# A Fourier filter feeding a two-layer product: 32 complex-product sums moved from GpSimd to VectorE, one step later

## The chip, the cores and the metric

The kernel runs on one core of a Trainium2 chip. Five engines work from their own instruction queues, each strictly in order, and wait for one another through semaphores: TensorE (PE in the profile; its weight loads are PEld), VectorE (DVE), ScalarE (ACT), GpSimd (POOL) and SyncE (SP), which here only issues transfers. Products are written to PSUM banks, which VectorE and ScalarE read; everything else lies in SBUF. The metric is the device time of one execution in microseconds (us).

## The reference

The input `x` is 8 batches of 3008 rows by 256 channels. The first half of the computation is a filter in the frequency domain, the second a two-layer product with a nonlinear step between:

```python
X = np.fft.rfft(x, axis=1)
Y = X * (filt_r + 1j * filt_i)[None]
y = np.fft.irfft(Y, n=3008, axis=1)
h = y.reshape(8 * 3008, 256) @ w_in          # 256 x 2048
out = (h - np.tanh(h)) @ w_out               # 2048 x 256
```

## The kernel before

**The transform.** 3008 is 64 times 47, and each transform is done as two small ones by matmul. `first` (line 338) does the 64-point part, `middle` (395) the 47-point part, the complex product with the filter and the 47-point part back, `last` (500) the 64-point part back. The batches go in five units: batch 0, the pairs (1, 2), (3, 4), (5, 6), and batch 7. Batch 0 is transformed in a prologue; every other unit is transformed piece by piece while the unit before it goes through the two-layer product. So `middle` of the first pair, unit 1, runs during the product of batch 0.

**One front step and one back step of `middle`.** For a pair there are 32 indices j. The front step of j (lines 424 to 448) multiplies a 128x512 tile `pz` on TensorE (L430). ScalarE makes `zs`, the two halves of `pz` swapped and one of them negated (L443, L444). VectorE makes `uv = pz * fr` (L445), GpSimd `zs = zs * fi` (L446) and then `uv = uv + zs` (L447). The back step `back()` of j multiplies `uv` again on TensorE into `pe` (L411), which ScalarE copies out (L414) and sends to memory. `uv` and `zs` have two buffers each. After the first index, fronts and backs alternate: front j, back j-1, front j+1, back j.

**The product.** Tokens come in groups of up to 512 columns, six groups for batch 0, and each group is worked through in four quarters of the 2048 hidden columns. A quarter is numbered U, and u is U modulo 4. Both products are done as two-by-two blocks with seven products and extra sums in place of eight products. In the round of quarter U, three things are interleaved: `up(U)` (532) forms the hidden tile `h` from the PSUM banks X, Y and Z; `shrink(U-1)` (607) applies the nonlinear step in two halves; `down(U-2)` (660) does the second product. The second half of `shrink` ends with a VectorE instruction (L633) and then `combine` (523): four GpSimd sums in a row, L524 to L527, that prepare the operand tiles of the second product. `last` of the next group uses the same `combine` lines for its tile `tu`.

**The order.** The schedule is written by hand: each engine takes its instructions in the order in which the Python code emits them. `up` has five places, called slots 0 to 4 here, where `t(k)` is called (for batch 0 these calls are lines 568, 578, 585, 594 and 602). A slot emits at most one step of `first` or `middle`, as the evenly spaced due times ask (line 1140); with u = 3, slots 0 and 2 are taken by `last` instead. The VectorE instructions of a round come in this order:

- slot 0, then L571 (the sum of Y and a copy of X), for u = 1 also L694, then L626 of the first half of `shrink`;
- slot 1, then L633 of the first half, for u = 1 also L700;
- slot 2, then L588, then L626 of the second half;
- slot 3, then L596 (the copy of X), then L633 of the second half, and with it the four GpSimd sums of `combine`; for u = 1 also L712;
- slot 4, then L604 (the sum into Z's share of `h`).

On TensorE, slot 1 lies behind the sixth product into X and slot 4 behind the fourth.

**The banks of the steps.** `pz`, `pe` and the other products of the steps have no bank of their own but take one of two, named "t" and "y" (line 1045). The bank "y" is also the Y of `up`:

```python
quarter, latest = [1], ["t"]
def zd(name, shape):
    latest[0] = "y" if quarter[0] in (1, 2, 3) and latest[0] == "t" else "t"
    return ps.tile(shape, F32, tag=latest[0], bufs=1, name=name)
```

`quarter[0]` is the number of the slot. A step in slot 0 or 4 takes "t", and the step in slot 1 then takes "y", which L571 must have read before.

Of the kernel before, what the change touches and what calls it, by code (L numbers as in the profile page):

```python
# [143 lines left out]
def kernel(  # L144
# [10 lines left out]
    V, G, ACT = nc.vector, nc.gpsimd, nc.scalar  # L155
# [13 lines left out]
    def dram(t, off, dims):  # L169
        return bass.AP(tensor=t, offset=off, ap=[list(d) for d in dims])  # L170
# [199 lines left out]
    def load_slots(j, pool=None):  # L370

        w = 4 * (128 + RP2)
        t = (tr.tile([IM + RP, 4, 128 + RP2], F32, tag="fg", bufs=2, name="fg") if pool is None else
             pool.tile([IM + RP, 4, 128 + RP2], F32, tag="a1", bufs=4, name="fg"))
        nc.sync.dma_start(t, fg_d[:, w * j:w * (j + 1)])
        return t[:, :, 0:128], t[:, :, 128:]

    def load_a2(p, j, filters=True, tag="a2"):

        t = tr.tile([RP2, 2 * BD], F32, tag=tag, bufs=2, name="a2")  # L380
        row = 32 * len(UNITS[p]) * DM
        nc.sync.dma_start(t, dram(ct1[p], 2 * j * BD, [[row, RP2], [1, 2 * BD]]))
        n = 2 if len(UNITS[p]) == 2 else 4
        if not filters:
            return t
        ft = tr.tile([128, 2, n, DM], F32, tag="ft", bufs=2, name="ft")
        for p0 in (0, IM):
            nc.sync.dma_start(ft[p0:p0 + IM], dram(filt_d, n * j * DM,
                                                   [[2 * NK * DM, IM], [NK * DM, 2], [1, n * DM]]))
        if n * (j + 1) == NK:  # L390
            nc.sync.dma_start(ft[IM:IM + 1, 0, n - 1, :],
                              dram(filt_r.tensor, SEQ // 2 * DM, [[DM, 1], [1, DM]]))
        return t, ft

    def middle(p, z):

        pair = len(UNITS[p]) == 2
        per = 1 if pair else 2
        n = NK // per
        w = BD // per  # L400
        a2 = {0: load_a2(p, 0)}
        mats = {0: load_slots(0)}
        waiting = []
        yield

        def back():
            j, uv = waiting.pop(0)
            pe = z("pe", [128, per, w])
            for i in range(per):
                k = per * j + i  # L410
                nc.tensor.matmul(pe[0:RP2, i], mats[k // 4][1][:, k % 4], uv[0:IM + RP, i],  # L411
                                 start=True, stop=True)
            e1 = tr.tile([RP2, 2, DM], F32, tag="e1", bufs=2, name="e1")
            ACT.copy(e1, pe[0:RP2])  # L414
            step = (NQ if pair else 2) * RP * DM
            ACT.dma_start(
                dram(ct2[p], per * j * RP2 * DM, [[DM, RP2], [step, 2], [1, DM]]), e1)

        for j in range(n):
            if j % 2 == 0 and j // 2 + 1 < n // 2:  # L420
                a2[j // 2 + 1] = load_a2(p, j // 2 + 1)
            k4 = per * j // 4
            if per * j % 4 == 0 and k4 + 1 < NK // 4:
                mats[k4 + 1] = load_slots(k4 + 1)
            pz = z("pz", [128, per, w])
            at, ft = a2[j // 2] if j % 2 == 0 else a2.pop(j // 2)
            for i in range(per):
                k = per * j + i
                lo = j % 2 * BD + i * w
                nc.tensor.matmul(pz[:, i], mats[k // 4][0][0:R2, k % 4],  # L430
                                 at[0:R2, lo:lo + w], start=True, stop=True)

            uv = tr.tile([128, per, w], F32, tag="uv", bufs=2, name="uv")
            zs = tr.tile([128, per, w], F32, tag="zs", bufs=2, name="zs")
            lo = j % 2 * per
            fr, fi = (ft[:, v, lo:lo + per, :] for v in range(2))
            if pair:
                fr, fi = (f.to_broadcast([128, 2, DM]) for f in (fr, fi))

            def rows(t):  # L440
                return t.rearrange("p i (b c) -> p (i b) c", c=DM)

            ACT.mul(zs[0:IM], pz[IM:128], -1.0)  # L443
            ACT.copy(zs[IM:128], pz[0:IM])  # L444
            V.tensor_mul(rows(uv), rows(pz), fr)  # L445
            G.tensor_mul(rows(zs), rows(zs), fi)  # L446
            G.tensor_add(uv, uv, zs)  # L447
            waiting.append((j, uv))
            yield
            if len(waiting) > 1:  # L450
                back()
                yield
        back()
        yield
# [401 lines left out]
    with tc.tile_pool(name="tr", bufs=2) as tr, tc.manual_schedule():  # L856
        with tc.tile_pool(name="pro", bufs=1) as pro, \
# [136 lines left out]
            for j in range(NK // 2):  # L994
# [13 lines left out]
                uv = tr.tile([128, 2, DM], F32, tag="uv", bufs=2, name="uv")  # L1008
                zs = tr.tile([128, 2, DM], F32, tag="zs", bufs=2, name="zs")
# [28 lines left out]
        with tc.tile_pool(name="dn", bufs=2) as dn, \  # L1038
# [48 lines left out]
            for U in range(total + 2):  # L1087
                i, u = divmod(U, 4)
                if U < total:
                    p, c = groups[i]  # L1090
# [36 lines left out]
                def t(k):  # L1127


                    nonlocal ms, done  # L1130
                    quarter[0] = k
                    if k == 2 and stores:
                        store(*stores.pop())
                    store_some(4)
                    if U >= total:
                        return
                    pos = 20 * c + 5 * u + k
                    if u == 3 and k in (0, 2) and i + 1 < len(groups):
                        next(lasts)
                    elif done < len(steps) and steps[done] <= pos:  # L1140
                        if done < n_f:
                            next(fs)
                        else:
                            next(ms)
                        done += 1
                        if done == n_f:
                            ms = middle(p + 1, z1)
                            next(ms)
                    next(late, None)
                    if U > 0 and k in (1, 3):  # L1150
                        next(copies, None)
# [56 lines left out]
```

## Time and profile before

| what | value |
|---|---|
| median of 3 runs (lowest to highest) | 2804.87 us (2803.72 to 2805.23) |
| the profiled execution: its time, its span | 2805.23 us, 2803.4 us |
| granted TensorE clock, mean over the span | 0.991 |
| busy share of the span: DVE, ACT, POOL | 68%, 67%, 63% |
| L445 in 240 to 480 us | 32 times, mean 686 ns |
| L446 in 240 to 480 us | 32 times, 47.5 us, mean 1483 ns |
| L447 in 240 to 480 us | 32 times, 59.5 us, mean 1861 ns |
| POOL idle before L524 in 240 to 480 us | 19.2 us, ended by L633 on DVE |

The 32 front steps of unit 1 lie between 238.8 and 467.1 us from the start of the span. A row of a timeline gives the start, the duration, the engine, the line, the tiles written and read, and in brackets the idle time of the engine before the row and what ended it. Matmuls are pipelined: a row of four 128x256 matmuls of which each starts 0.216 us after the one before is listed with 1.03 us, since the end of the last is counted too. TensorE is packed if the next row starts where this rate puts it, and the time lost is what the next row starts later. Each matmul of the code appears as two in the trace.

### The profile page before, as it was taken

Reading aid. Unit: us, or ns where it says so; the run is one execution under the profiler, and the core shown is the slowest. Engines: PE = TensorE matmul, PEld = TensorE weight load, DVE = VectorE, ACT = ScalarE, POOL = GpSimd, SP = SyncE. Lnnn points to the kernel's source line nnn. Section 1 sums busy time; section 2 is a strip of 40 time slices with the busy share of each in tenths; the row PEclk is TensorE's granted clock in tenths of the full one; section 3 lists DMA queues with packets and bytes.
Section 4 is the critical chain, followed back from the end, with each engine's and each line's share of the span. In section 5 each row is a group of like instructions: output and inputs, shape, how many; then the busy total and the mean of one; then the engine's idle time right before and its main releaser. Section 6 shows DMA issues by size and latency. Waiting matters only on the chain.

```text
span 2803.4 us, 36463 instructions
## 1 busy us (share of the span) xinstructions
PE 2715.9 (97%) x12438; PEld 2273.4 (81%) x12438; DVE 1912.5 (68%) x2175; ACT 1885.6 (67%) x2790; POOL 1767.5 (63%) x1407
## 2 busy tenths in 40 slices
PE   4799999999999999999999999999999999999998
PEld 2577778888888888888888888888888888898887
DVE  6756666566776777666677776766676676777776
ACT  2476777666767776666677777666666676666665
POOL 5546887544776777544576777654476666565655
PEclk7999999999999999999999999999999999999999
DMA  9754443322333222223323233112223222111010
GB/s 251 208 189 122 106 124 76 91 83 72 75 79 77 73 71 59 63 79 81 87 72 75 70 80 83 38 43 65 59 66 83 60 57 58 29 19 26 16 23 17
DMA packets 322591, 217.53 MB, mean 78 GB/s; under 512 B 224782, under 2 KB 274746, under 8 KB 322156
## 3 DMA queue, kind: packets, MB, share of 16 engines
q1 hardware_dynamic: 266826, 157.28, 23.6%
q10 hardware_dynamic: 52818, 51.53, 6.0%
q0 software_dynamic: 2752, 6.30, 0.8%
q8 instruction: 100, 1.64, 0.2%
q14 instruction: 95, 0.78, 0.1%
HBM read 138.87 MB, written 79.17 MB: 78 GB/s over the span
## 4 chain that ended last, share of the span: by engine, by line
PE 83%; DVE 5%; ACT 4%; DMA 3%; POOL 2%; issue 2%; ACTq 0%; SPq 0%; DVEq 0%; POOLq 0%
PE o L680 35%; PE x L545 21%; PE z L545 10%; PE y L545 5%; PE pe L411 3%; PE pz L430 3%; PE pu L511 3%; PE pf L351 2%; DVE h L626 2%; ACT y L622 1%; DVE h L596 1%; DMA raw<-in_moe_w_in_dram 1%; DMA filt<-in_filt_r_dram 1%; ACT y L619 1%; DVE h L633 0%
## 5 line engine op out<-in xcount | busy, mean ns | idle before, releaser
L626 DVE TENSOR_TENSOR h<-h,y 128x1024 f32<-128x1024 f32 (+2 forms) x384 | 577.4, 1504 | 311.5 <-ACT y L622 310.4
L680 PE MATMUL o<-t,wd 128*128 128x256 f32 (+2 forms) x3072 | 775.1, 375 | 1.8 <-POOL t L526 1.3
L680 PEld LDWEIGHTS o<-t,wd 128*128 128x128 f32 x3072 | 579.9, 190 | 92.9 <-issue 22.0
L633 DVE SCALAR_TENSOR_TENSOR h<-sq,h 128x1024 f32<-128x1024 f32 (+2 forms) x384 | 558.7, 1455 | 121.0 <-ACT sq L630 113.0
L524 POOL TENSOR_TENSOR t<-h 128x512 f32<-128x512 f32 (+2 forms) x192 | 240.2, 1251 | 552.0 <-DVE h L633 401.3
L545 PE MATMUL x<-tu,wu 128*128 128x256 f32 (+2 forms) x2304 | 582.4, 375 | 4.3 <-POOL tu L525 2.2
L680 PE MATMUL o<-h,wd 128*128 128x256 f32 (+2 forms) x2304 | 582.5, 375 | 4.0 <-DVE h L633 4.0
L545 PEld LDWEIGHTS x<-tu,wu 128*128 128x128 f32 x2304 | 430.9, 190 | 104.7 <-issue 42.4
L680 PEld LDWEIGHTS o<-h,wd 128*128 128x128 f32 x2304 | 430.7, 190 | 76.9 <-issue 15.8
L630 ACT ACTIVATE sq<-y,near_b 128x1024 f32<-128x1024 f32 (+2 forms) x384 | 435.0, 1133 | 6.4 <-DVE h L633 0.2
L619 ACT ACTIVATE y<-h 128x1024 f32<-128x1024 f32 (+2 forms) x384 | 397.4, 1035 | 14.4 <-ACT e L414 6.4
L622 ACT ACTIVATE y<-y 128x1024 f32<-128x1024 f32 (+2 forms) x384 | 399.9, 1041 | 6.6 <-ACT a L352 0.4
L551 ACT COPY s<-x 128x512 f32<-128x512 f32 (+2 forms) x192 | 110.8, 577 | 328.5 <-PE x L545 308.4
L527 POOL TENSOR_TENSOR t<-t,h 128x512 f32<-128x512 f32 (+2 forms) x192 | 318.9, 1661 | 0.1
L551 ACT COPY u<-x 128x512 f32<-128x512 f32 (+2 forms) x384 | 220.7, 575 | 138.2 <-PE x L545 119.9
L525 POOL TENSOR_TENSOR t<-h,t 128x512 f32<-128x512 f32 (+2 forms) x192 | 246.0, 1281 | 15.1
L526 POOL TENSOR_TENSOR t<-h 128x512 f32<-128x512 f32 (+2 forms) x191 | 245.6, 1286 | 0.0
L446 POOL TENSOR_TENSOR zs<-zs,ft 128x512 f32<-128x512 f32 x112 | 164.8, 1472 | 91.4 <-ACT zs L444 91.2
L447 POOL TENSOR_TENSOR uv<-uv,zs 128x512 f32<-128x512 f32 x112 | 206.7, 1846 | 9.1 <-DVE uv L445 0.5
L545 PE MATMUL x<-ut,wu 128*128 128x256 f32 (+2 forms) x768 | 198.6, 381 | 10.0 <-DVE h L596 8.3
L588 DVE TENSOR_TENSOR h<-z,u 128x512 f32<-128x512 f32 (+2 forms) x192 | 128.8, 671 | 112.6 <-ACT u L551 111.6
L545 PE MATMUL z<-tu,wu 128*128 128x256 f32 (+2 forms) x768 | 194.5, 376 | 0.0
(122 smaller groups left out, 3291.6 us busy)
## 6 DMA issues: line engine op xcount, KB each, us to landing
a<-ct SPq DMA_DIRECT2D x64, 384.0 KB, 3.8
ft<-filt SPq DMA_DIRECT2D x96, 256.0 KB, 4.5
out_dram<-ot SPq DMA_DIRECT2D x1392, 16.0 KB, 1.5
ct<-e ACTq DMA_DIRECT2D x112, 192.0 KB, 2.2
ct<-a ACTq DMA_DIRECT2D x80, 256.0 KB, 2.9
x_sb<-in_x_dram SPq DMA_DIRECT2D x69, 256.0 KB, 2.9
e<-ct SPq DMA_DIRECT2D x33, 512.0 KB, 4.3
fg<-fg SPq DMA_DIRECT2D x40, 392.0 KB, 4.9
```

The lines of the kernel that those rows point to most:

```text
L524: G.tensor_sub(t[0], b[0][1], b[0][0])
L525: G.tensor_sub(t[1], b[1][1], t[0])
L526: (V if shared else G).tensor_sub(t[2], b[1][1], b[0][1])
L527: G.tensor_sub(t[3], t[1], b[1][0])
L545: nc.tensor.matmul(bank[:, k], wu[:, q - 1, (2 * u + k) * 128:(2 * u + k + 1) * 128], rhs[q - 1], start=(first and k == 0), stop=True, ski ...
L551: ACT.copy(t, X)
L619: ACT.activation(y[k], ht[k], AF.Arctan, scale=S)
L622: ACT.activation(y[k], y[k], AF.Square, accum_out=y_sums[:, 2 * U + k // 2:2 * U + k // 2 + 1])
L626: V.tensor_mul(ht[k], ht[k], y[k])
L630: ACT.activation(sq[k], y[k], AF.Square, bias=near_b, scale=A)
L633: V.scalar_tensor_tensor(out=ht[k], in0=sq[k], scalar=K, in1=ht[k], op0=ALU.add, op1=ALU.mult)
L680: nc.tensor.matmul(product(q), wd[:, q - 1, (2 * u + k) * 128: (2 * u + k + 1) * 128], rhs[q - 1][:, k], start=(u == 0 and k == 0 and q == ...
```

## The change

In `middle` of unit 1 alone, GpSimd no longer adds `zs` to `uv`. The sum is kept back and emitted on VectorE: at the end of the next back step or, for the very first index, which has no back step after it, at the end of the second front step. The sums of the other units stay where they were.

```diff
@@ middle(p, z)
         waiting = []
+        late_add = p == 1
+        adds = []
         yield
...
             V.tensor_mul(rows(uv), rows(pz), fr)
             G.tensor_mul(rows(zs), rows(zs), fi)
-            G.tensor_add(uv, uv, zs)
+            if not late_add:
+                G.tensor_add(uv, uv, zs)
             waiting.append((j, uv))
+            if adds:
+                V.tensor_add(*adds.pop())
+            if late_add:
+                adds.append((uv, uv, zs))
             yield
             if len(waiting) > 1:
                 back()
+                if adds:
+                    V.tensor_add(*adds.pop())
                 yield
```

## The prediction

> **What bounds the kernel now.** I read the page first: busy shares, then the chain that ended last.
>
> ```profile
> PE 2715.9 (97%) x12438; PEld 2273.4 (81%) x12438; DVE 1912.5 (68%) x2175; ACT 1885.6 (67%) x2790; POOL 1767.5 (63%) x1407
> PE 83%; DVE 5%; ACT 4%; DMA 3%; POOL 2%; issue 2%; ACTq 0%; SPq 0%; DVEq 0%; POOLq 0%
> ```
>
> TensorE sets the time. A change on POOL and DVE counts only where TensorE then waits more or less than now. The change acts where the first pair's `middle` runs, 240 to 480 us, so I read the windows (busy time of PE, PEld, DVE, ACT, POOL) there and in the next stretch, and what TensorE waits for there.
>
> ```profile
> 240.00:480.00 240.00, 234.46 (x979) 179.19 (x978) 154.66 (x173) 175.10 (x267) 194.52 (x142) 1.00 0.44 113
> 480.00:720.00 240.00, 239.73 (x1119) 205.89 (x1118) 152.61 (x171) 162.52 (x240) 116.79 (x99) 1.00 0.29 78
> ```
> ```profile
> PE pe L411 <- POOL uv L447: 3.9, 2, 3.3
> PE pe L411 <- DVE h L571: 1.3, 6, 0.3
> ```
>
> POOL is the fullest of the helpers (194.5 of 240), yet TensorE waits for it twice only, at the first back step and near the end (470.16). Against the rate of 0.216 us a matmul these cost 3.48 and 0.72 us. So 4.2 us is all that a faster sum can give directly. The six waits for L571 are the second thing to see: a step in slot 1 uses bank "y" and cannot start until L571 has read it.
>
> Next, the timelines of TensorE, POOL and DVE at the start of round 9, the first round with u = 1 (start, duration, engine, line).
>
> ```profile
> 264.82 1.03 PE L545 MATMUL x<-tu,wu 128*128 128x256 f32 x4
> 265.69 1.02 PE L430 MATMUL pz<-a,fg 94*128 94x512 f32 x2
> 266.55 1.03 PE L545 MATMUL z<-tu,wu 128*128 128x256 f32 x4
> ```
> ```profile
> 260.73 1.27 POOL L524 TENSOR_TENSOR t<-h 128x512 f32<-128x512 f32 x1 [2.89 <-DVE h L633]
> 262.08 1.27 POOL L525 TENSOR_TENSOR t<-h,t 128x512 f32<-128x512 f32 x1
> 263.31 1.27 POOL L526 TENSOR_TENSOR t<-h 128x512 f32<-128x512 f32 x1
> 264.55 1.27 POOL L527 TENSOR_TENSOR t<-t,h 128x512 f32<-128x512 f32 x1
> 265.78 1.26 POOL L446 TENSOR_TENSOR zs<-zs,ft 128x512 f32<-128x512 f32 x1
> 267.12 1.27 POOL L447 TENSOR_TENSOR uv<-uv,zs 128x512 f32<-128x512 f32 x1
> ```
> ```profile
> 261.78 0.68 DVE L604 TENSOR_TENSOR h<-z,u 128x512 f32<-128x512 f32 x1
> 262.51 0.69 DVE L571 TENSOR_TENSOR h<-y,s 128x512 f32<-128x512 f32 x1
> 266.81 0.42 DVE L694 TENSOR_TENSOR o<-o,p 128x256 f32<-128x256 f32 x1 [3.61 <-ACT p L693]
> 267.15 2.32 DVE L626 TENSOR_TENSOR h<-h,y 128x1024 f32<-128x1024 f32 x1
> ```
>
> TensorE is packed here: 264.82, 265.69, 266.55 follow without a hole. The front step in slot 4 of round 8 put its POOL product (L446) behind the four sums of `combine`, emitted in that round's slot 3. It ends only at 267.04; DVE passes L571 at 262.51.
>
> **The change, part by part.**
>
> *Removed from POOL:* 32 sums, 59.5 us in the window. Worth 4.2 us at most, the two waits.
>
> *Added to DVE:* 32 sums of 128x512 with both inputs in SBUF. The trace has no such row. L445, as large, takes 0.69 us and the next instruction starts 0.61 later (261.17 to 261.78); L626, twice the size with both inputs in SBUF, takes 1.22 alone and hands over after 1.15 (273.39 to 274.54). I take 0.61. The bounds: 0.42, a 128x256 sum (L694), and 0.69 plus one POOL instruction of 1.27, because L626 beside L447 waited that one out:
>
> ```profile
> 256.57 1.27 POOL L447 TENSOR_TENSOR uv<-uv,zs 128x512 f32<-128x512 f32 x1
> ```
> ```profile
> 256.83 2.09 DVE L626 TENSOR_TENSOR h<-h,y 128x1024 f32<-128x1024 f32 x1 [0.31 <-ACT y L622]
> 258.84 0.68 DVE L596 COPY h<-x 128x512 f32<-128x512 f32 x1
> ```
>
> *The place of the sums.* Each waits for its own L446 and holds DVE until then. The step moves past the back step's matmul, ScalarE copy and the store issued on ScalarE; no transfer moves, and neither SP nor POOL gets a new wait.
>
> - Slots 1 to 4 (27 sums): L446 is done or nearly done, and L626 loses the POOL sum that slowed it, 2.09 to about 1.22. In round 8, slot 3, DVE then runs L626 256.83, sum 257.98, L596 258.59 instead of 258.84. Where L626 was not slowed (290.73, 1.20 us), L596 ends at 293.1 and X is needed at 294.09. The sums in slot 1 stand before L633, which waits for ScalarE (316.87 for L626, 319.85 for L633). In slot 4 they delay L604, whose bank is refilled about 5 us later. I cost these at nothing; the cover is this slack, 1 us before L596, and if it went, each would cost up to 0.9 (1.88 minus 1.0).
> - Slot 0 of rounds 9, 13, 17 and 21 (u = 1): the sum stands before L571, L694 and L626. In round 9 it starts where L447 did, 267.12; L571 starts at 267.73 and ends at 268.42; the matmul follows 0.14 later (as 282.68 to 282.82), at 268.56 instead of 265.69: 2.87. The four POOL sums start 0.26 earlier, as L596 and so L633 do (the 0.25 above, rounded with the handover): 2.61. Round 13 the same (333.97; `pz` 332.54): 2.60. Round 17 (400.87; 399.45): 2.59. Round 21 (468.10; L571 0.62; 466.09) 3.38, less 0.45 because L626 in round 20 took 2.27: 2.93, and the 0.72 wait that followed it goes: 2.21. DVE's own 3.61 us of idle before L694 hides the wait from L694 and L626, but TensorE needs L571 long before that.
> - The first index: its sum stands in slot 0 of round 8 before L571. L446 ends at 246.82 and POOL goes straight to the next L446. If the sum slips in ahead, `pe` starts at 248.34 instead of 249.22 (gain 0.9); if it waits that product out, L571 ends near 249.3 and `pe` starts about 0.2 late. I take the second, since POOL needs no signal between its two products.
>
> *Sum:* 2.61 + 2.60 + 2.59 + 2.21 + 0.2 = 10.2 us on the profiled execution of 2805.23 (span 2803.4). That run lies 0.36 above the median, so 2804.87 + 10.2 = 2815.1. What waits on TensorE elsewhere follows it and shifts along.
>
> [...] POOL's sum takes 1861 ns on the mean, DVE's product 686. [...]
>
> **The rivals.**
>
> 1. *No wait at L571* (not slower): the POOL waits go and nothing takes their place: -4.2, 2800.7; with the waits for L571 (six of about 0.37) and three of 0.36 behind L596 gone as well, -7.6, 2797.3. It decides if L446 ends before DVE reaches slot 0, at 262.5. It ends 4.5 us later and the sums before it start only after L633. Chance 0.07.
> 2. *The wait is there but hits no one:* if the step in slot 1 held bank "t", L571 could be late. Then only the ends change: 0.2 minus 0.72, 2804.4. Against it, the six waits of `pe` for L571. Chance 0.04.
> 3. *DVE becomes the bound:* the other sums do not hide. With the POOL block, seven in slot 3 at 0.9 give 6.3 more, 2821; all 27 others at 0.61 give 16.5, 2832. For it, L626 already suffers from POOL; against it, DVE is at 64% and loses the neighbour that slowed it. Chance 0.10.
>
> **How the numbers follow.** Forecast 0.79. Its own bounds: a sum of 0.42 (-0.8), twice the head start (-1.2), a gain at the first index (-1.1) give 7.1; a POOL block at each of four sites (+5.1) and no head start (+1.2) give 16.5. The range 2809 to 2820 leaves rivals 1 and 2, most of 3 and the far end of the forecast out, about 0.2. A measurement of this kernel can tell 0.2% (5.6 us). Rival 1 gives faster 0.03 and no change 0.04, rival 2 no change 0.04; the rest is slower, 0.89.
>
> **What would show it.** In the changed profile: four waits of `pz` (L430 before, a few lines lower after) for L571, about 2.6 us each, one per group; DVE idle about 4.5 us before the new sum in slot 0, ended by POOL's L446; no wait of TensorE for the POOL sum; L626 near 1.2 to 1.4; PE busy in the same stretch of work 6 us or more below its length. The forecast is wrong if those four waits are missing, or if TensorE waits behind L596 or L633 instead.

## The result and the profile after

The changed kernel takes 2820.7 us (median of 6 runs, 2819.3 to 2821.2) against 2805.6 us for the kernel before (6 runs, 2803.7 to 2812.2): the ratio is 1.0050, with a 95% interval of 1.0037 to 1.0063. That is 15.1 us more, by the interval 10.4 to 17.7. The direction and the mechanism came as forecast. The size did not quite: 10.2 us were forecast, and 2820.7 lies 0.7 us above the upper end of the range. The profiled executions show the same, 2821.2 against 2805.23 us.

In the changed kernel's file the lines have moved a little: L411 is now L414, L430 L433, L446 L449, L571 L581, L626 L636; the new sum is L461, and L454 for the first index. In the other runs they differ again by a few lines. The page of the changed kernel, its first line and its chain:

```profile
PE 2723.6 (97%) x12438; PEld 2278.4 (81%) x12438; DVE 1923.2 (68%) x2207; ACT 1886.2 (67%) x2790; POOL 1706.5 (61%) x1375
PE 73%; DVE 4%; ACT 3%; issue 2%; POOL 1%; ACTq 0%; DVEq 0%; POOLq 0%
```

POOL has lost 61 us of work and DVE has gained 11 us, and the kernel is slower: neither share says anything about the time. In the stretch of the change, taken to 492 us here since its work ends later (the columns are the busy times of PE, PEld, DVE, ACT and POOL, then the granted TensorE clock, the DMA share and GB/s), and in what TensorE waits for there:

```profile
240.00:492.00 252.00, 238.22 (x968) 180.80 (x967) 164.49 (x203) 173.40 (x264) 131.15 (x107) 0.98 0.42 106
```
```profile
PE pz L433 <- DVE h L581: 9.5, 4, 2.5
PE pe L414 <- DVE h L581: 3.9, 4, 3.4
```

POOL falls from 194.5 to 131.2 us, and TensorE no longer waits for it. In its place stand four waits of `pz` for L581 (L571 before), one in each round with u = 1. Beside them there is something that no line of the profile before had in this stretch: a granted clock of 0.98, not 1.00.

The start of round 9 on TensorE, POOL and DVE (start, duration, engine, line):

```profile
267.43 1.03 PE L555 MATMUL x<-tu,wu 128*128 128x256 f32 x4
270.67 1.12 PE L433 MATMUL pz<-a,fg 94*128 94x512 f32 x2 [2.22 <-DVE h L581]
271.63 1.55 PE L555 MATMUL z<-tu,wu 128*128 128x256 f32 x4
272.98 1.06 PE L690 MATMUL o<-h,wd 128*128 128x256 f32 x2
```
```profile
266.79 1.28 POOL L537 TENSOR_TENSOR t<-t,h 128x512 f32<-128x512 f32 x1
268.02 1.27 POOL L449 TENSOR_TENSOR zs<-zs,ft 128x512 f32<-128x512 f32 x1
```
```profile
269.32 0.69 DVE L461 TENSOR_TENSOR uv<-uv,zs 128x512 f32<-128x512 f32 x1 [4.31 <-POOL zs L449]
269.93 0.68 DVE L581 TENSOR_TENSOR h<-y,s 128x512 f32<-128x512 f32 x1
270.53 0.42 DVE L704 TENSOR_TENSOR o<-o,p 128x256 f32<-128x256 f32 x1
270.86 1.22 DVE L636 TENSOR_TENSOR h<-h,y 128x1024 f32<-128x1024 f32 x1
```

DVE stands idle for 4.31 us in front of the sum, L581 comes behind it, and `pz` 0.06 us after L581 has ended. Then comes what was not forecast: from 271.63 the same matmuls take 1.55 and 1.06 us where they took 1.03 and 0.60 before. The second of these before:

```profile
267.41 0.60 PE L680 MATMUL o<-h,wd 128*128 128x256 f32 x2
```

Three stretches of the changed kernel show why; the figure behind the busy times is the granted clock:

```profile
251.52:254.93 3.41, 3.41 (x10) 2.70 (x9) 1.23 (x2) 2.91 (x4) 0.00 (x0) 0.50 1.02 235
272.00:275.41 3.41, 3.41 (x10) 2.70 (x9) 1.42 (x3) 3.37 (x5) 1.27 (x1) 0.50 0.23 52
411.95:415.36 3.41, 3.41 (x10) 2.70 (x9) 1.42 (x2) 3.37 (x5) 1.27 (x1) 0.50 0.22 47
```

After three of the five long waits the granted clock is 0.50 for 3.41 us, and each of these stretches shows TensorE as fully busy.

**Where the time went.** Both kernels give TensorE the same 12438 matmuls in the same order, so the start of the same matmul in the two traces tells how far the changed kernel is behind. At 233.4 us it is 0.85 us behind, at 494.8 us 14.61, and that stays within 0.05 until 2716 us. The change thus cost 13.8 us in this stretch and nothing later. The other 2.2 us of the 16.0 between the two profiled executions lie in the prologue and at the very end. The change does not act there, and the prologue differs between executions of one kernel: in the first run of the experiments the changed kernel is 0.81 us ahead of the kernel before at 233.4 us. Taken apart, with the time lost against the rate of 0.216 us a matmul (each of the four waits includes 0.10 us that the second matmul of `pz` starts late behind it):

| step of the sum | forecast, us | measured, us |
|---|---|---|
| first back step (3.48 us of wait before, 3.58 now) | +0.2 | +0.1 |
| waits for L571 in rounds 9, 13, 17, 21 | +2.61, +2.60, +2.59, +2.93 | +2.48, +2.62, +2.61, +2.80 |
| wait of the back step in round 21 that goes | -0.72 | -0.79 |
| shorter waits for L571 and L596 elsewhere | 0 | about -1.1 (the rest of the balance) |
| halved clock, three stretches | not in the sum | +1.68, +1.68, +1.68 |
| sum | +10.2 | +13.8 |

### The profile page after: what moved, and what is told of

The parts are those of the page before. It is cut to its first block, busy times and chain, and to the rows that moved or that the text cites. A ratio compares the mean times of both kernels' runs of the same rounds, so it can differ in the third digit from the quotient of the medians.

```text
span 2819.4 us, 36471 instructions
## 1 busy us (share of the span) xinstructions
PE 2723.6 (97%) x12438; PEld 2278.4 (81%) x12438; DVE 1923.2 (68%) x2207; ACT 1886.2 (67%) x2790; POOL 1706.5 (61%) x1375
## 4 chain that ended last, share of the span: by engine, by line
PE 73%; DVE 4%; ACT 3%; issue 2%; POOL 1%; ACTq 0%; DVEq 0%; POOLq 0%
PE o L690 32%; PE x L555 19%; PE z L555 9%; PE y L555 5%; PE pu L521 3%; PE pe L414 2%; PE pz L433 2%; DVE h L636 2%; PE pf L351 1%; ACT y L632 1%; DVE h L606 1%; ACT y L629 0%; DVE ot L740 0%; PE pf L361 0%; DVE h L643 0%
## 5 line engine op out<-in xcount | busy, mean ns | idle before, releaser
L636 DVE TENSOR_TENSOR h<-h,y 128x1024 f32<-128x1024 f32 (+2 forms) x384 | 568.9, 1482 | 311.9 <-ACT y L632 310.8
L643 DVE SCALAR_TENSOR_TENSOR h<-sq,h 128x1024 f32<-128x1024 f32 (+2 forms) x384 | 552.4, 1438 | 110.8 <-ACT sq L640 102.3
L535 POOL TENSOR_TENSOR t<-h,t 128x512 f32<-128x512 f32 (+2 forms) x192 | 246.9, 1286 | 15.1
L449 POOL TENSOR_TENSOR zs<-zs,ft 128x512 f32<-128x512 f32 x112 | 159.1, 1421 | 128.6 <-ACT zs L447 119.4
L555 PE MATMUL x<-ut,wu 128*128 128x256 f32 (+2 forms) x768 | 198.5, 381 | 10.5 <-DVE h L606 8.3
L555 PE MATMUL y<-ut,wu 128*128 128x256 f32 (+2 forms) x768 | 193.7, 375 | 0.0
```

Of the source, the lines that this page charges most:

```text
L535: G.tensor_sub(t[1], b[1][1], t[0])
L555: nc.tensor.matmul(bank[:, k], wu[:, q - 1, (2 * u + k) * 128:(2 * u + k + 1) * 128], rhs[q - 1], start=(first and k == 0), stop=True, ski ...
L636: V.tensor_mul(ht[k], ht[k], y[k])
L643: V.scalar_tensor_tensor(out=ht[k], in0=sq[k], scalar=K, in1=ht[k], op0=ALU.add, op1=ALU.mult)
```

## The experiments

The theory: the loss comes from four sums alone, because of where they stand (behind `combine` on POOL, before L571 on DVE) and because slot 1 needs the bank that L571 reads; the halved clock is a consequence of these waits. The rivals: the number of sums moved, or VectorE's load; and a clock that falls for reasons of its own. The kernels of one heading below ran on one chip, beside the kernel before.

### The change again, its four sums alone, its banks, its place

**The changed kernel once more** (no edit).

> The changed kernel once more, beside the others of this series. Theory: TensorE waits for L571 behind the late sum in rounds 9, 13, 17 and 21 (10.3 us together in the first profile of the changed kernel), and after three of its five long waits the granted clock fell to a half for 3.41 us, about 1.65 us each. So +14 to +16 us on the kernel before if the clock falls again after three waits; +10 to +12 if after none, +17 to +19 if after all five. Rival, the sums on VectorE cost by their number: the same total, but no tie to those four places.

Measured: 2818.8 us against 2805.6, ratio 1.0047 (1.0034 to 1.0061), +13.2 us, the 14 to 16 lying inside the interval. The profile has the same four waits, 9.5 us in all, and again three drops of the clock to 0.50, the first twice as long (6.80 us from 247.60, the others 3.40 from 271.50 and 411.40).

**Only the four sums of slot 0 moved.**

```diff
+            late_add = p == 1 and quarter[0] == 4 and U % 4 == 0
             if not late_add:
                 G.tensor_add(uv, uv, zs)
```

> Only the four sums that stand in slot 0 of rounds 9, 13, 17 and 21 go to VectorE a step later; the other 28 stay on GpSimd as before. Theory: the four waits are there in full, 2.4 to 3.4 us each, 10 to 12 us, and with zero to four drops of the clock at 1.65 us each the kernel is 10 to 18 us slower than before. Rival, the cost goes with the number of sums moved: an eighth of it, about +2 us.

Measured: 2821.3 us, ratio 1.0053 (1.0039 to 1.0067), +15.7 us. Four sums of 32 carry the whole loss. What TensorE waits for between 235 and 495 us:

```profile
PE pz L433 <- DVE h L582: 10.7, 4, 3.1
PE pe L414 <- POOL uv L452: 3.3, 1, 3.3
PE pe L414 <- DVE h L582: 1.3, 6, 0.3
```

By the starts of the matmuls the four waits are 2.63, 2.72, 2.73 and 3.25 us, 0.2 to 0.55 us longer than with all sums moved (2.38, 2.52, 2.51 and 2.70). POOL still adds beside DVE here. In the kernel before, L626 took 2.09 us beside such a sum in round 8, against 1.23 with all sums moved; that puts `combine` later. The granted clock was 0.50 in four stretches of 3.35 us each, from 248.65, 269.05, 340.75 and 412.45.

**Other banks in rounds with u = 1.**

```diff
                 latest[0] = "y" if quarter[0] in (1, 2, 3) and latest[0] == "t" else "t"
+                if 8 < U < 24 and U % 4 == 1:
+                    latest[0] = "y" if quarter[0] in (2, 3) else "t"
```

> The changed kernel with one thing different: in rounds 9, 13, 17 and 21 the steps take other banks, slot 1 bank t, slots 2 and 3 bank y. The late sum still waits for GpSimd in front of L571 on VectorE. Theory, the wait reaches TensorE only because the step in slot 1 needs bank y from L571: the four waits go, and with them the drops of the clock that followed them; what stays is the wait at the first back step (3.6 us as before, perhaps with one drop of 1.7). -2 to +2 us on the kernel before. [...]

Measured: 2805.5 us, ratio 1.0002 (0.9993 to 1.0011). Nothing is left of the loss, although DVE waits for POOL as long as in the changed kernel:

```profile
264.21 0.69 DVE L461 TENSOR_TENSOR uv<-uv,zs 128x512 f32<-128x512 f32 x1 [4.48 <-POOL zs L449]
264.82 0.68 DVE L581 TENSOR_TENSOR h<-y,s 128x512 f32<-128x512 f32 x1
```
```profile
262.14 1.03 PE L555 MATMUL x<-tu,wu 128*128 128x256 f32 x4
263.01 1.02 PE L433 MATMUL pz<-a,fg 94*128 94x512 f32 x2
263.87 1.03 PE L555 MATMUL z<-tu,wu 128*128 128x256 f32 x4
```

DVE is idle for 4.48 us, L581 starts only at 264.82, and yet `pz` starts at 263.01, right behind the matmuls before it. The wait reaches TensorE through the bank and in no other way.

**The sums of slot 0 behind L571.** They are put aside and emitted just before L626, in rounds 8, 9, 13, 17 and 21.

```diff
-                    V.tensor_add(*adds.pop())
+                    late_sum(adds.pop())
...
         e()
+        while held:
+            V.tensor_add(*held.pop())
         shrinks(1)
```

> All 32 sums stay on VectorE; those that fell into slot 0 (rounds 8, 9, 13, 17, 21) are emitted behind L571 and, in rounds with u = 1, L694, just before L626. Theory, the place before L571 is the whole loss: no wait for L571 beyond the 0.3 us ones, the first back step starts 0.5 to 1.7 us earlier than in the changed kernel, and the time is -3 to +1 us on the kernel before. Rival, the engine and not the place costs: +10 us or more stays.

Measured: 2803.7 us, ratio 0.9993 (0.9984 to 1.0002): the loss is gone with all 32 sums on VectorE. What TensorE waits for between 235 and 495 us:

```profile
PE pe L422 <- DVE uv L592: 2.8, 1, 2.8
PE pe L422 <- DVE h L589: 0.5, 3, 0.2
```

The first back step still waits 2.8 us, now for its sum, and the granted clock was 0.50 in the 6.60 us from 246.10.

### The clock, the other 28 sums, and two edits that gain

**Useless products in the waits.** In slot 1 of the five rounds, TensorE multiplies constants into the bank "t", which is free there; nothing reads the result.

```diff
         if close:
+            for _ in range({8: 7, 9: 5, 13: 5, 17: 5, 21: 5}.get(U, 0)):
+                fill = ps.tile([128, 2, 128], F32, tag="t", bufs=1, name="fill")
+                nc.tensor.matmul(fill, wf1[:, 0], wf1, start=True, stop=True)
             t(1)
```

> The changed kernel, and in slot 1 TensorE gets useless products of the constant weights into the idle bank t just before the step that has to wait: seven 128x256 ones in round 8 (3.0 us at full clock) and five (2.2 us) in each of rounds 9, 13, 17 and 21. They fall into time that TensorE spends waiting for L571 anyway, and nothing reads them. Theory, the halved clock is a consequence of these waits: no half clock between 240 and 490 us, and more work makes the kernel 4 to 6 us faster than the changed one, +9 to +11 us on the kernel before; the four waits for L571 shrink to under 0.6 us each in the profile since the useless products take their place. Rival, the clock falls for another reason, or the five windows cost nothing: +14 us or more stays.

Measured: 2821.2 us, ratio 1.0046 (1.0033 to 1.0060). The granted clock over the whole execution was 0.991, as in the kernel before (0.991) and not 0.989 as in the changed one; that is in line with the theory, but the gain failed to come. The products were too long: seven took 4.97 us (247.50 to 252.47), 0.71 each where 0.43 was reckoned (why is open), and so they outlasted the waits:

```profile
246.63 1.03 PE L555 MATMUL x<-tu,wu 128*128 128x256 f32 x4
247.50 5.14 PE L590 MATMUL fill<-wf_sb 128*128 128x256 f32 x14
252.47 1.02 PE L414 MATMUL pe<-uv,fg 112*96 112x512 f32 x2
```

This run decides nothing on the price; a later one, with fewer products, does.

**The four sums back on GpSimd, the other 28 on VectorE.**

```diff
+            late_add = p == 1 and not (quarter[0] == 4 and U % 4 == 0)
             if not late_add:
                 G.tensor_add(uv, uv, zs)
```

> The changed kernel with the four sums of slot 0 in rounds 9, 13, 17 and 21 back on GpSimd, right behind their product; the other 28 stay on VectorE. Theory, those four carry the loss alone: no wait of pz for L571, -2 to +2 us on the kernel before (the upper part if the clock falls after the first back step's wait). Rival, the 28 others carry a share by their number: +7 us or more stays.

Measured: 2805.6 us against 2805.5, ratio 0.9997 (0.9988 to 1.0006). No wait of `pz` is left between 235 and 495 us:

```profile
PE pe L414 <- DVE h L582: 3.9, 4, 3.4
```

The 28 cost nothing, and bring nothing, within 0.1%.

**The first index on VectorE as well.** To the sums behind L571 is added:

```diff
+            own = late_add and j == 0
-            G.tensor_mul(rows(zs), rows(zs), fi)
+            (V if own else G).tensor_mul(rows(zs), rows(zs), fi)
+            if own:
+                V.tensor_add(uv, uv, zs)
...
```

> All sums on VectorE, those of slot 0 behind L571 (as in the run that emitted them there), and for the very first index also the product with the imaginary part, with its sum right behind it, on VectorE, so that the first back step no longer waits for the four sums of combine. Theory, the 3.5 us wait at the first back step goes to about 0.4, so -3 to -6 us on the kernel before. Rival, the first back step then waits for something else, ScalarE or L571: -1 to +1 us.

Measured: 2801.4 us against 2805.5, ratio 0.9983 (0.9974 to 0.9992). By the starts of the same matmuls 3.2 us of it come at the first back step, which no longer waits.

**And `uv` of a front in slot 0 behind L571.**

```diff
-            V.tensor_mul(rows(uv), rows(pz), fr)
+            if late_add and quarter[0] == 0:
+                held.insert(0, (V.tensor_mul, rows(uv), rows(pz), fr))
+            else:
+                V.tensor_mul(rows(uv), rows(pz), fr)
...
```

> The same, and the product uv of a front step in slot 0 is emitted behind L571 as well, so that L571 no longer stands behind a product that waits for ScalarE. Theory, the six waits for L571 of about 0.37 us go too: -5 to -8 us on the kernel before, the best of all. Rival, the product is then late for its own sum and the gain is given back: no better than the version without it.

Measured: 2798.8 us, ratio 0.9972 (0.9961 to 0.9982). No wait of TensorE is listed any more between 235 and 495 us, and it is busy for 249.8 of the 250 us from 240:

```profile
240.00:490.00 250.00, 249.81 (x1074) 196.79 (x1073) 176.81 (x218) 186.27 (x286) 148.42 (x117) 1.00 0.44 111
```

### The price of the clock, and what the moved sums are worth

**Fewer useless products.**

```diff
-            for _ in range({8: 7, 9: 5, 13: 5, 17: 5, 21: 5}.get(U, 0)):
+            for _ in range({8: 4, 9: 3, 13: 3, 17: 3, 21: 3}.get(U, 0)):
```

> As the run with useless products, but fewer, since each took 0.71 us there and not 0.43 and five outlasted the wait: four in round 8 (2.8 us for a wait of 3.6) and three in rounds 9, 13, 17 and 21 (2.1 us for waits of 2.4 to 2.9). Theory, the halved clock follows the idle stretches and costs what the changed kernel has beyond its waits: no half clock between 240 and 490 us, the same +10 us of lost places at the four steps, and 3 to 5 us less than the changed kernel. Rival, no gain: +14 us or more on the kernel before stays, and the half clock had no price of its own.

**The changed kernel on the same chip** (no edit).

> The changed kernel beside the run with fewer useless products: +13 to +16 us on the kernel before, with two to four drops of the clock between 240 and 490 us.

Measured: 2814.8 us with the products (1.0030, 1.0019 to 1.0041) and 2821.3 without (1.0051, 1.0037 to 1.0064), against 2806.4 for the kernel before. TensorE does 16 products more and the kernel is 6.5 us faster. The four steps lose their place as before (2.52, 2.51, 2.51 and 2.69 us later than the rate puts them), but the products fill most of that time, so the waits that are left are short:

```profile
PE pz L433 <- DVE h L581: 1.8, 4, 0.6
PE pe L414 <- DVE h L581: 1.2, 4, 0.6
```

The stretch from 240 to 490 us differs in the granted clock, first with the products, then without:

```profile
240.00:490.00 250.00, 245.91 (x1013) 184.43 (x1012) 165.53 (x206) 175.00 (x267) 133.16 (x109) 1.00 0.43 108
```
```profile
240.00:490.00 250.00, 236.15 (x953) 178.06 (x952) 161.92 (x198) 172.30 (x263) 130.49 (x106) 0.97 0.42 106
```

By the starts of the same matmuls, the stretch from 233.4 to 494.8 us costs 9.4 us more than in the kernel before with the products, and 15.0 without. The halved clock is worth the difference, 5.5 us in that pair. This is a net price: in the changed kernel a short wait for L596 shrinks by 0.37 us behind the halved stretch at 272.00, and by 0.11 in round 13, which has none.

**The two edits that gain, with the sums left on GpSimd.** The kernel before, with the first index's product and sum on VectorE and the products `uv` of slot 0 behind L571; in slot 0 the GpSimd sum is then emitted after them.

```diff
+            own, hold = p == 1 and j == 0, p == 1 and quarter[0] == 0
...
+            if hold:
+                held.insert(0, (G.tensor_add, uv, uv, zs))
+            else:
+                (V if own else G).tensor_add(uv, uv, zs)
...
```

> The kernel before, all sums on GpSimd but that of the first index, with the two edits of the best version: the first index's product and sum on VectorE, and the product uv of fronts in slot 0 behind L571 (the sum on GpSimd is then emitted behind it). Theory, moving the sums to VectorE brings almost nothing of its own, the two edits bring 3.5 and about 2 us: -4 to -6 us on the kernel before, within 2 us of the best version. Rival, the moved sums bring the gain: -2 us or less.

Measured: 2798.3 us against 2806.4, ratio 0.9974 (0.9966 to 0.9983). The long wait of the first back step is gone here too:

```profile
PE pe L413 <- POOL uv L456: 0.7, 3, 0.2
```

That is as fast as the best version with 32 sums on VectorE (0.9972, on another chip). Both beat the kernel before and the changed one; the other 31 sums may stay where they were.

## Why the prediction was right, and where it fell short

- **The four waits.** Right, place by place and in size: 10.7 us forecast, 10.5 measured. Each link was shown by taking it away: the sum's place before L571 (sums behind it, -0.07%), the bank (+0.02%), the four sums alone (+0.53%, all of the loss), the other 28 (-0.03%). The sum starts where the forecast put it, with the end of POOL's product (269.29 and 269.32 in round 9). The condition of the prediction's rival 2, bank "t" for the step in slot 1, is what the run with other banks brought about: 2805.5 us, near the 2804.4 that this rival gave.
- **The head start of the POOL sums.** Right: it shortens the four waits by 0.25, 0.20, 0.22 and 0.55 us, against the run with four sums alone; 0.26, 0.27, 0.27 and 0.45 were taken.
- **The first index.** Right in its choice. The new sum (here L454) met POOL's next product and took 1.73 us, not 0.69, and the wait grew from 3.48 to 3.58 us.
- **The sums in slots 1 to 4 at nothing.** Right, and rival 3 is refuted by the run with 28 sums on VectorE. The 31 sums behind the first took 0.83 us on the mean, between the 0.69 and the blocked 1.96 of the bounds. L626 (now L636) took 1.41 us on the mean, at the edge of the 1.2 to 1.4 forecast, and 1.69 before.
- **What POOL's sums were worth.** At most 4.2 us, said the prediction; without the four misplaced sums it came to 0.03%, within the interval of nothing. The long wait at the first back step is not the sum's doing alone: `pe` was due at 245.74, POOL's product, behind `combine`, ended only at 246.82, and its sum at 249.16. With the sum alone on VectorE the wait stayed (3.58 us in the changed kernel, 2.8 behind L571); with the product there as well it went. (In rival 1, the terms given for -7.6 add up to -7.5.)
- **The sum's missing term.** The step that failed is the last sentence of the sum, "What waits on TensorE elsewhere follows it and shifts along": it took the rate of TensorE after a wait to be the rate before it. Three waits of 2.4 to 3.6 us were each followed by 3.41 us at a granted clock of 0.50, 5.0 us lost in all, and that is why 2820.7 lies above the range. The waits elsewhere that grew shorter, which the sum left out as well, gave back about 1.1 us. The terms that the sum did have are borne out by the run with fewer useless products: it keeps the four waits, has no halved clock and costs 9.4 us in this stretch, where 10.2 were forecast.
- **What would have shown it.** The signs named beforehand are there: four waits of `pz`, 4.3 and 4.45 us of DVE idle before the sum in the rounds looked at, no wait of TensorE for POOL's sum, and TensorE busy for 13.8 us less than the 252 of the stretch. The granted clock was not among them.

## What to carry to other kernels

Where an engine takes its instructions in the order emitted, as DVE did here (idle for 4.31 us before the sum, with L581 behind it), a moved instruction takes its waits with it to its new place: ask first what stands behind it there, who needs that, and when what it waits for ends in the trace; its own duration (0.83 against 1.86 us here) decided nothing. Where the order is the trouble, another order is the cure: two small moves past L571 and `combine` gained 0.26% with 31 of the 32 sums left on the slower engine. And a wait on the bounding engine may cost more than its length, here 1.68 us more behind three of five: look at the granted clock in the stretch behind it.

## What the hardware showed beyond expectation

A wait of TensorE of 2.38 us (2.22 us of idle in the profile) was followed by half the granted clock: in the changed kernel the clock is 0.50 for 3.41 us from 251.52, 272.00 and 411.95 us, behind idle of 3.42, 2.22 and 2.35 us. By the starts of the same matmuls each of these stretches cost 1.68 us, before what shorter waits give back: its matmuls start about 0.43 us apart, not 0.216.

The length of the wait alone does not say whether a drop follows. Idle of 2.36 us before 341.30 and of 2.54 us before 481.29, both longer than two of the three above, was followed by none: the granted clock is 1.00 from 341.30 to 345.00 and from 481.29 to 485.00. The first back step of the kernel before waits 3.32 us, and the clock is 1.00 from 247.87 to 254.70. At that step the run with other banks and the run with the four sums back on GpSimd both wait 3.4 us: the first shows a clock of 1.00 over 240 to 490 us, the second 0.50 from 248.10 to 251.40. What decides between them is open.

That the drops go with the waits is what the runs without long waits show: with the waits filled to 0.6 us or less by useless products, and with no wait listed at all in the best version, the granted clock over 240 to 490 us is 1.00, against 0.97 for the changed kernel on the chip of the first of these.
